# The first batch of a retention kernel: pairs of heads over 512 tokens in place of groups of four heads over 256

## The chip, the cores and the metric

The kernel runs on one core of one Trainium2 chip. Its time is the device time of one execution in microseconds (us). Before the change three runs gave a median of 301.55 us (301.51 to 302.88).

## The reference

A multi-head retention layer is followed by a feed-forward layer. There are 8 batches, 8 heads, 576 tokens and a head size of 64, all in float32.

```python
scores = q @ k.T / sqrt(64)                       # per batch and head, 576 x 576
gamma  = 1 - 2.0 ** (-5 - head)
ret    = scores * (gamma ** (i - j) if i >= j else 0)
attn   = ret @ v                                  # 576 x 64
x      = attn, heads side by side                 # 4608 x 512
h      = x @ w_in                                 # 4608 x 2048
g      = where(h > 0, h, exp(min(h, 0)) - 1)
out    = g @ w_out                                # 4608 x 512
```

Since the decay is a product of a factor of the query's position and one of the key's, q and k are scaled by those factors once. The sequence is then cut into chunks: inside a chunk the masked scores are multiplied with v, and what lies ahead of a chunk comes in through a state, the sum of (scaled k) x v over the earlier tokens, a 64 x 64 matrix for each head.

## The kernel before

All matmuls take bf16 and add up in float32. `w_in` and `w_out` are loaded once, with a cast to bf16 in the transfer, by eight transfers of 512 columns or rows each (`load_w_in`, `load_w_out`), which GpSimd (POOL) issues. All loads of q, k and v and all stores are issued by SyncE (SP).

An *item* is 256 tokens (`T` = 0 or 1) of four heads (`w` = 0 or 1) of one batch, so that a batch has four items for its first 512 tokens; the last 64 tokens of four batches at a time are handled as two tail items. In items 0 to 11 a partition holds two neighbouring tokens (512 B runs in memory); from item 12 on one token (256 B runs). An item goes through these steps, named as in the code:

- `ldq`, `ldk`, `ldv`: loads of 256 KB (`load_main`, L405).
- `cq`, `ck`: scaling with the decay factors in halves, one for each of the two tokens of a partition (`scaled`, L476), on DVE or POOL; `cv`: cast of v (`cast_v`, L511).
- `T`, `cp`: for the first items, four TensorE transposes for q and four for k (L524) and a copy from PSUM (`turn_pe`, L530).
- `sc`: scores in chunks of 64 partitions, as 64x64 tiles of the array (`do_scores`); `mask`: causal mask on DVE (L851).
- `st`: two state increments, one for each 64-partition chunk (`do_state`); `mid`, `end`: running sums of them on DVE or ACT (L748 to L757); `bm`, `be`: these sums laid out as block-diagonal bf16 matrices (L765, L779).
- `iv`: queries times states and masked scores times v, in one PSUM accumulation (`do_inter`, `do_values`); `xc`: two copies to the transposed activations `xt` (`put_x`, L907).

A *block* is what the feed-forward layer takes at once. The first three batches (`NARROW`) have two blocks of 256 tokens each, the others one of 512; the tails are one more. `ffn1` multiplies `xt` with `w_in` (a narrow operation does two columns of 128 with 256 tokens each, a wide one 128 columns with 512 tokens), then ACT takes the exponential (L1045), ACT or DVE the maximum with 0 (L1053, L1055), and DVE joins both to `g` (L1060). `ffn2` multiplies `g` with `w_out`; the result is copied and stored.

The order of all this is not written by hand. Each step is an `Op` with dependencies, a rank and an estimated cost on each engine that may run it, and `Plan.run` lays them out on the engines when the kernel is built; the instructions are then issued in that order, and every engine works through its own in order. Constants steer it: `FROM` holds the earliest times at which the eight weight transfers may be issued, `HOLD` makes the loads from item 4 on wait for a piece of the weights (a one-element memset on POOL, L414, which waits for the transfer and which the load waits for), `ON` fixes engines, `RANKS` shifts ranks. The first two blocks' `ffn1` are planned together, four operations of each to a piece of `w_in`. TensorE begins with ten matmuls of zeros (`emit_warm`), and where the plan has a gap before 50 us, the code that issues the instructions puts matmuls or transposes of zeros into it (L1219).

The decay factors come from positions (`pos_i`, iota on POOL), `expo` (DVE, L298) and three exponentials on ACT (`emit_factors`, L1148), ahead of the first item. The causal mask of the items is built on POOL (L317).

Of the kernel before, what the change touches and what calls it, by code (L numbers as in the profile page):

```python
# [36 lines left out]
class Plan:  # L37
# [30 lines left out]
    def run(self, began):  # L68
# [58 lines left out]
        while len(order) < len(self.ops) or any(wire.values()) or events:  # L127
# [53 lines left out]
            for e, h in heads.items():  # L181
                h[1] -= step * rate[e]
                if h[1] < 1e-6:
                    wire[e].pop(0)
                    lanes[e] -= 1
                    heapq.heappush(events, (now + LEAVE, next(count), h[2]))
# [7 lines left out]
ENTER, LEAVE = 1.25, 0.55  # L194


LEAD = 64
HOLD = {4: "wi0"}
RANKS = {}
TOGETHER = 1  # L200
# [7 lines left out]
FROM = (8.96, 10.28, 13.13, 15.23, 17.0, 17.0, 17.44, 17.82)  # L208
ON = {'mid1': 'DVE', 'be2': 'DVE', 'md_1_0': 'ACT', 'xc1_2': 'DVE', 'cv0': 'DVE', 'md_1_1': 'ACT', 'cq12': 'DVE'}
DIRECT = True  # L210
# [5 lines left out]
TWO = False  # L216
# [18 lines left out]
def kernel(  # L235
# [45 lines left out]
    for h in range(H):  # L281
        nc.vector.memset(lgt[:, h : h + 1], lg[h])
    pos_i = const.tile([P, NU], I32, name="pos_i")
    nc.gpsimd.iota(pos_i[:, :FT].rearrange("p (t e) -> p t e", e=2), pattern=[[2 * P, 2], [1, 2]], base=-MID,
                   channel_multiplier=2)
    nc.gpsimd.iota(pos_i[:ST, FT:], pattern=[[0, 1]], base=FT * P - MID, channel_multiplier=1)
    nc.gpsimd.iota(pos_i[ST:, FT:], pattern=[[0, 1]], base=MID - FT * P, channel_multiplier=-1)
    pos = const.tile([P, NU], FP32, name="pos")
    nc.vector.tensor_copy(pos, pos_i)
# [3 lines left out]
    nc.vector.memset(bk, 0.0)  # L293
    bt = const.tile([P, 1], FP32, name="bt")
    nc.vector.memset(bt[:ST], math.log(scale))
    nc.vector.memset(bt[ST:], 0.0)
    expo = const.tile([P, NU, H], FP32, name="expo")
    nc.vector.tensor_tensor(  # L298
        expo,
        pos.unsqueeze(2).to_broadcast([P, NU, H]),  # L300
        lgt.unsqueeze(1).to_broadcast([P, NU, H]),
        ALU.mult,
    )
# [8 lines left out]

    mask = const.tile([P, 2, 2, C], BF16, name="mask")
    nc.vector.memset(mask, 1.0)
    for c in range(2):
        m = mask[c * C : (c + 1) * C]
        nc.gpsimd.affine_select(out=m, in_=m, compare_op=ALU.is_ge, fill=0.0, base=0,  # L317
                                pattern=[[-1, 2], [1, 2], [2, C]], channel_multiplier=-2)
    mask_t = const.tile([P, ST], BF16, name="mask_t")
    nc.vector.memset(mask_t, 1.0)  # L320
# [3 lines left out]
    nc.vector.memset(diag[D:, 1:], 1.0)  # L324

# [20 lines left out]
    for b in ORDER:  # L346
        for r in range(FT if isinstance(b, int) else 1):
# [4 lines left out]
            else:  # L352
                it.b, it.T, it.w = b, r // 2, r % 2
                it.blk = 2 * b + it.T if b < NARROW else 2 * b
# [903 lines left out]
```

## Time and profile before

| | |
|---|---|
| median of three runs | 301.55 us |
| the profiled execution | 301.8 us, of which the span from its first to its last instruction 300.1 us |
| TensorE matmuls busy | 291.5 us (97%) |
| ScalarE (ACT) busy | 188.2 us (63%) |
| VectorE (DVE) busy | 172.3 us (57%) |
| GpSimd (POOL) busy | 164.4 us (55%) |
| HBM read and written | 36.70 MB, 9.44 MB |
| first `ffn1` matmul | at 19.06 us |
| first `ffn1` matmul of batch 1 | at 50.40 us |
| granted TensorE clock | 1.00 |

The profile is of one execution; all times in it count from its first instruction. In lists of instructions a line has start, length, engine, line of the kernel, operation, output and input names, shape and number; a bracket behind it names idle time of the engine just before and what ended it. PE is TensorE, DVE VectorE, ACT ScalarE, POOL GpSimd, SP SyncE; PEld is the loading of weights into the array, which overlaps with matmuls. A "q" behind an engine is its instruction queue. Lengths of matmuls in a row are modelled and reach a little past the start of the next ones, so that the start times are the better measure. In a table of windows the columns are the stretch, its length and busy time of PE, PEld, DVE, ACT and POOL, then TensorE clock, share of the DMA engines and GB/s.

### The profile page before, as it was taken

How to read it: one execution, taken by the hardware profiler on the slowest of the kernel's cores; microseconds unless marked ns; L12 is line 12 of the kernel's file. 1: busy time of each engine (PE TensorE's matmuls, PEld its weight loads, DVE VectorE, ACT ScalarE, POOL GpSimd, SP SyncE). 2: the span in 40 equal slices, each digit the busy share in tenths (PEclk: the TensorE clock that was granted, in tenths of full speed). 3: DMA queues.
4: the chain of work that ended last, by engine and by line, in shares of the span. 5: the costliest groups of instructions: out<-in, count | busy, mean ns of one | idle time of the engine just before them, and what ended most of it. 6: DMA issues, size and time to landing. Idle time of an engine off the chain costs nothing.

```text
span 300.1 us, 8496 instructions
## 1 busy us (share of the span) xinstructions
PE 291.5 (97%) x3367; PEld 169.5 (56%) x3402; DVE 172.3 (57%) x312; ACT 188.2 (63%) x365; POOL 164.4 (55%) x292
## 2 busy tenths in 40 slices
PE   8899999999999999999999999999999999999996
PEld 4678746768767764545544554554545444444444
DVE  4888934948865537696843675646442474334300
ACT  2439724838766656786776667676764686777611
POOL 5790389984988849598794888579330000000000
DMA  6999999999998998999999999976761101011132
GB/s 201 272 207 210 226 292 316 231 260 184 179 238 183 217 205 193 219 191 212 192 224 165 173 231 208 186 176 106 175 142 72 35 0 38 35 35 37 35 106 70
DMA packets 135607, 50.10 MB, mean 167 GB/s; under 512 B 108176, under 2 KB 131088, under 8 KB 135568
## 3 DMA queue, kind: packets, MB, share of 16 engines
q1 hardware_dynamic: 131344, 45.37, 71.0%
q0 software_dynamic: 4224, 4.19, 8.4%
q8 instruction: 26, 0.43, 0.6%
q14 instruction: 13, 0.11, 0.1%
HBM read 36.70 MB, written 9.44 MB: 154 GB/s over the span
## 4 chain that ended last, share of the span: by engine, by line
PE 92%; DMA 2%; SPq 2%; issue 1%; POOL 1%; DVE 0%; ACT 0%; ACTq 0%
PE f L269 89%; PE sc L269 3%; DMA rqk<-in_q_dram 2%; SPq L405 2%; POOL qkn L476 1%; PE f L524 1%; POOL w_in_sb L454 0%; DVE xt L907 0%; ACT ot L1094 0%; ACTq L1094 0%
## 5 line engine op out<-in xcount | busy, mean ns | idle before, releaser
L1060 DVE SCALAR_TENSOR_TENSOR g<-e,f 128x512 bf16<-128x512 f32 x144 | 96.3, 685 | 79.3 <-ACT f L1053 78.7
L269 PE MATMUL f<-w_out_sb,g 128*128 128x512 bf16 (+2 forms) x582 | 136.9, 367 | 2.7 <-issue 1.9
L269 PE MATMUL f<-xt,w_in_sb 128*128 128x256 bf16 (+1 forms) x759 | 138.8, 325 | 0.6 <-DVE xt L907 0.2
L1045 ACT ACTIVATE e<-f 128x512 f32<-128x512 f32 x144 | 85.4, 596 | 48.0 <-PE f L269 41.6
L269 PEld LDWEIGHTS <-w_in_sb 128*128 128x128 bf16 x768 | 74.1, 98 | 53.2 <-DVE xt L907 0.5
L269 PEld LDWEIGHTS <-g 128*128 128x128 bf16 x608 | 56.7, 98 | 58.3
L1053 ACT ACTIVATE f<-f 128x512 f32<-128x512 f32 x122 | 72.2, 593 | 0.0
L818 POOL TENSOR_TENSOR s_mid<-mid,diag 128x256 bf16<-128x256 f32 x60 | 35.6, 613 | 12.9 <-DVE mid L807 7.9
L1094 ACT COPY ot<-f 128x512 f32<-128x512 f32 (+2 forms) x38 | 21.4, 566 | 22.6 <-PE f L269 22.6
L476 POOL TENSOR_TENSOR qkn<-rqk,far_q 128x256 bf16<-128x256 f32 x40 | 23.8, 613 | 5.5 <-DMA rqk<-in_q_dram 5.4
L476 POOL TENSOR_TENSOR qkn<-rqk,far_k 128x256 bf16<-128x256 f32 x40 | 23.9, 613 | 0.4 <-DMA rqk<-in_k_dram 0.2
L511 POOL CAST vn<-rv 128x512 bf16<-128x512 f32 x28 | 17.0, 610 | 7.3 <-DMA rv<-in_v_dram 7.3
L476 POOL TENSOR_TENSOR qkn<-rqk,gq 128x256 bf16<-128x256 f32 x21 | 13.1, 635 | 12.1 <-DMA rqk<-in_q_dram 12.1
L907 ACT CAST xt<-f 128x256 bf16<-128x256 f32 x24 | 9.2, 425 | 14.1 <-PE f L269 14.1
L851 DVE TENSOR_TENSOR pt<-sc,mask 128x1024 bf16<-128x1024 f32 x12 | 14.6, 1219 | 4.3 <-PE sc L269 4.2
L845 DVE TENSOR_TENSOR pt<-sc,mask_t 128x1024 bf16<-128x1024 f32 (+1 forms) x12 | 12.5, 1042 | 5.7 <-PE sc L269 4.2
L1055 DVE TENSOR_SCALAR f<-f 128x512 f32<-128x512 f32 x22 | 15.2, 695 | 0.9 <-ACT e L1045 0.6
L579 POOL TENSOR_TENSOR qkt<-rqt,gq 128x256 bf16<-128x256 f32 x16 | 9.5, 613 | 10.6 <-DMA rqt<-in_k_dram 10.6
L883 ACT CAST xt<-f 128x512 bf16<-128x512 f32 x16 | 8.6, 589 | 10.2 <-PE f L269 9.5
L476 POOL TENSOR_TENSOR qkn<-rqk,gk 128x256 bf16<-128x256 f32 x22 | 13.3, 621 | 2.4 <-DMA rqk<-in_k_dram 2.4
L818 POOL TENSOR_TENSOR s_end<-end,diag 128x256 bf16<-128x256 f32 x20 | 12.3, 613 | 0.4 <-DVE end L807 0.3
L807 DVE TENSOR_TENSOR mid<-f,mid 128x256 f32<-128x256 f32 (+1 forms) x24 | 9.1, 380 | 2.5
(81 smaller groups left out, 170.7 us busy)
## 6 DMA issues: line engine op xcount, KB each, us to landing
out_dram<-ot SPq DMA_DIRECT2D x30, 256.0 KB, 3.0
rqk<-in_q_dram SPq DMA_DIRECT2D x40, 128.0 KB, 3.4
rqk<-in_k_dram SPq DMA_DIRECT2D x40, 128.0 KB, 3.3
rv<-in_v_dram SPq DMA_DIRECT2D x40, 128.0 KB, 3.1
rqk<-in_q_dram SPq DMA_DIRECT2D x12, 256.0 KB, 5.8
rqk<-in_k_dram SPq DMA_DIRECT2D x12, 256.0 KB, 5.4
rv<-in_v_dram SPq DMA_DIRECT2D x12, 256.0 KB, 6.9
w_in_sb<-in_moe_w_in_dram POOLq DMA_DIRECT2D x4, 512.0 KB, 8.8
```

The source lines that it names most:

```text
L269: pin(nc.tensor.matmul(*a, **kw))
L476: pin(alu[op.eng].tensor_tensor(tiles[key][:, i, e], tiles[raw][:, :, e], g, ALU.mult))
L511: pin(copy[op.eng](tiles["vn", n], tiles["rv", n]))
L579: pin(alu[op.eng].tensor_tensor(tiles["qkt", n, m, j][:, hs], tiles["rqt", n, m, j][:, hs], g[:, hs], ALU.mult))
L818: pin(alu[op.eng].tensor_tensor(tiles[out].rearrange("p h (j d) -> p h j d", j=2), tiles[key][:, i].unsqueeze(2).to_broadcast([P, 2, 2, D] ...
L845: pin(nc.vector.tensor_tensor(tiles[it.pt].rearrange("p i h n -> p (i h n)")[:, : 2 * w * C].rearrange("p (i x n) -> p i x n", i=2, n=C), ...
L851: pin(nc.vector.tensor_tensor(tiles["pt", n].rearrange("p i h n -> p (i h) n"), tiles[it.sc].rearrange("p i (h n) -> p (i h) n", h=2), mas ...
L1045: pin(nc.scalar.activation(tiles[ekey], tiles[hkey], AF.Exp))
L1053: pin(nc.scalar.activation(ph, ph, AF.Relu))
L1055: pin(nc.vector.tensor_scalar_max(ph, ph, 0.0))
L1060: pin(nc.vector.scalar_tensor_tensor(tiles[gkey], tiles[ekey], -1.0, tiles[hkey], ALU.add, ALU.min))
L1094: pin(copy[op.eng](tiles[okey][:, :cols], tiles[pkey][:, :cols]))
```

## The change

The first 512 tokens of batch 0 are cut in another way. Its four items are now the four pairs of heads, each over all 512 tokens, with four neighbouring tokens in a partition (1 KB runs). Everything that they do is new (`quad`):

- Scaling is still in halves, of two tokens to a partition each. The factors are those of `quad_pos` (four positions for a partition), computed ahead of the first item; those of the other batches, and their mask, are built by steps of their own (`near_i`, `near_x`, `near_f`, `mask_n`) that batch 1 waits for.
- A chunk is 32 partitions (128 tokens). Scores take 32 matmuls for 16, with 64 rows and 32 columns of the array each; the mask `quad_m` has four rows of 32 partitions.
- The states are summed over the chunks by TensorE: four running sums in one PSUM tile, over 32, 64, 96 and 128 partitions, in 40 matmuls for 16 (a part of 96 partitions is made of 64 and 32), with a drain of TensorE ahead of the last eight. One copy (`sm`) takes the four sums to bf16; `mid`, `end` and `bm` of these items are gone. `be`, on POOL, is now needed for the tail only.
- Values take 32 matmuls with 32 rows and 64 columns each; the three states of chunks 1 to 3 come in by six matmuls with 64 rows, half a head pair each; a drain stands ahead of the last 16.
- Two copies put an item into `xt`, for one pair of heads over 512 tokens.

Batch 0 is thus one block of 512 tokens: wide `ffn1`, four row groups in `ffn2` (two at a time, `OPEN`), and a store in which a row group has every fourth token. The loads come in the order of `SEQ`. The weights may be issued from other times (`FROM`; the first piece from 7.2 in place of 8.96), the loads of batch 1 wait for the first piece of `w_out` in place of `w_in` (`HOLD`), seven warm-up matmuls stand for ten, and the fillers are of 512 columns where a gap is long. `RANKS` and `ON` get many entries; the estimate of transfers gets a lag (`LAG`).

```diff
-HOLD = {4: "wi0"}
-RANKS = {}
-TOGETHER = 1
+HOLD = {4: 'wo0'}
+RANKS = {'ck04': 3, 'cp(5, 0)': -1, 'st4b1': -8, 'xc0_4': 0.5, 'iv4b0': 0.5, ...}
+OPEN = 2
...
+SEQ = 'q0 k0 q1 k1 v0 q2 k2 v1 q3 k3 v2 v3'
+WARM = 7
+WEIGHTS = "wi0 wi1 wi2 wi3 wo0 wo1 wo2 wo3"
...
-FROM = (8.96, 10.28, 13.13, 15.23, 17.0, 17.0, 17.44, 17.82)
-ON = {'mid1': 'DVE', 'be2': 'DVE', 'md_1_0': 'ACT', 'xc1_2': 'DVE', 'cv0': 'DVE', ...}
+FROM = (7.2, 7.9, 12.0, 16.3, 9.9, 12.3, 6.3, 18.0)
+ON = {'be3': 'ACT', 'cv2': 'ACT', 'cp(1, 0)': 'ACT', 'cp(2, 1)': 'ACT', 'cq12': 'DVE', ...}
...
+            if it.early:
+                def emit_quad(op, src=src, key=key):
+                    pin(nc.sync.dma_start(
+                        tiles[key].rearrange("p a b d -> p (a b d)").rearrange("p (h r) -> p h r", h=2),
+                        src[0, 2 * it.j : 2 * it.j + 2, : FT * P, :].rearrange("h (p e) d -> p h (e d)", e=4)))
...
+            if it.early:
+                es = slice(2 * e, 2 * e + 2)
+                pin(alu[op.eng].tensor_tensor(
+                    by_token(tiles[key][:, i])[:, es], by_head(tiles[raw])[:, :, es].rearrange("p h e d -> p e h d"),
+                    (quad_q, quad_k)[i][:, es, 2 * it.j : 2 * it.j + 2].unsqueeze(3).to_broadcast([P, 2, 2, D]), ALU.mult))
+                return
...
+    def quad(it):
...
+        def emit_sc(op):
+            tt = tiles["qkT", n]
+            for m in range(4):
+                for i in range(2):
+                    for cs in chunk:
+                        mm(tiles[sc_key][cs, i, m * P : (m + 1) * P].rearrange("p (e t) -> p e t", e=4),
+                           tt[half[i], 7 - m, cs], tt[half[i], 0:4, cs], start=True, stop=True)
...
+        def emit_st(op):
+            o, kn, vn = tiles[skey], by_token(tiles["qkn", n][:, 1]), by_head(tiles["vn", n])
+            for kind, lo, hi in ((0, 0, 1), (1, 0, 2), (2, 0, 2), (3, 0, 4), (2, 2, 3)):
+                rows = slice(lo * QC, hi * QC)
+                if lo:
+                    pin(nc.tensor.drain())
+                for e in range(4):
+                    for i in range(2):
+                        acc(skey, 0, i, o[half[i], kind * D : (kind + 1) * D], kn[rows, e, i], vn[rows, i, e])
...
+            def values(cs):
+                for m in range(4):
+                    for c in cs:
+                        for i in range(2):
+                            acc(xkeys[c % 2], 0, i, tiles[xkeys[c % 2]][half[i], c // 2 * P : (c // 2 + 1) * P],
+                                vn[chunk[c], i, 3 - m], pt[chunk[c], i, m * P : (m + 1) * P])
+
+            values((0, 1))
+            for c in (1, 2, 3):
+                for i in range(2):
+                    acc(xkeys[c % 2], 0, i, tiles[xkeys[c % 2]][half[i], c // 2 * P : (c // 2 + 1) * P].rearrange(
+                        "p (e t) -> p e t", e=4), sums[half[i], j, c - 1], tt[half[i], 0:4, chunk[c]])
+            pin(nc.tensor.drain())
+            values((2, 3))
...
+    def emit_near_f(op):
+        pin(nc.scalar.activation(gq[:, :FT], expo[:, :FT], AF.Exp, bias=bq))
+        pin(nc.scalar.activation(gk, expo[:, :FT], AF.Exp, bias=bk, scale=-1.0))
+        pin(nc.scalar.activation(gq[:, FT], expo[:, FT], AF.Exp, bias=bt))
...
     def emit_warm(op):
-        for _ in range(10):
+        for _ in range(WARM):
             mm(tiles["warm"], zero[:, :P], zero, start=True, stop=True)
...
+    pieces = WEIGHTS.split()
+    for n, (name, t) in enumerate(zip(pieces, FROM)):
+        named[name].at = t
+        if n:
+            named[name].turn.append(named[pieces[n - 1]])
```

More of the change, by code (lines that the diff above doesn't have):

```diff
@@ L215 @@
 AWAY = {}
-TWO = False
 LAST = (0, 256, 384, 512)
@@ L1124 @@
         far_ready[0].at = 22.0
-    for it in items:
+    for word in SEQ.split():
+        load_main(items[int(word[1])], word[0])
+    for it in items[FT:]:
         (load_tail if it.tail else load_main)(it)
```

235 lines of the change are left out of this document (152 added, 83 removed).

## The prediction

> **What bounds the kernel now.** I read the page first: busy shares, slices, chain.
>
> ```profile
> PE 291.5 (97%) x3367; PEld 169.5 (56%) x3402; DVE 172.3 (57%) x312; ACT 188.2 (63%) x365; POOL 164.4 (55%) x292
> ...
> PE 92%; DMA 2%; SPq 2%; issue 1%; POOL 1%; DVE 0%; ACT 0%; ACTq 0%
> ```
>
> TensorE is the bound. But its 97% contain matmuls of zeros that fill waits, so I listed its instructions in order of time up to 40 us.
>
> ```profile
> 1.26 4.28 PE L269 MATMUL f<-zero 128*128 128x512 bf16 x10 [1.26 <-DVE zero L274]
> ...
> 15.78 1.07 PE L1219 MATMUL f<-ident,zero 128*128 128x128 bf16 x16
> ...
> 19.06 1.05 PE L269 MATMUL f<-xt,w_in_sb 128*128 128x256 bf16 x8
> ...
> 20.61 1.38 PE L269 MATMUL f<-xt,w_in_sb 128*128 128x256 bf16 x11
> 22.19 10.33 PE L269 MATMUL f<-xt,w_in_sb 128*128 128x256 bf16 x93 [0.21 <-DVE xt L907]
> ```
>
> The reader is to see two regimes. Before 19 us TensorE works in bits between fillers (operand zero): the attention of the first four items. From 22.19 us it is dense: the chain from there to the end holds no wait longer than 0.2 us ahead of the last output copies. So time is saved or lost where the dense stretch begins, or where something tears a hole into it. In 22.19 to 34.33 us lie 109 narrow matmuls less one group of transposes (0.22): 0.109 each. The 19 run earlier are worth 2.1 us, so the first FFN1 stands as if it had begun at 22.19 - 2.1 = 20.1 us.
>
> What sets that start is in the chain in order of time:
>
> ```profile
> 7.04 7.02 DMA rqk<-in_q_dram
> 14.06 0.07 issue
> 14.13 0.85 POOL qkn L476
> 14.98 0.75 POOL w_in_sb L454
> 15.73 0.02 issue
> 15.76 1.22 POOL qkn L476 x2
> ```
>
> The last item's q lands at 14.06; its k is scaled from 15.76, behind an issue of weights on POOL; FFN1 follows. Landings (issue plus time to landing, asked for each load): k of item 0 4.5, q of item 1 7.2, q and k of item 2 9.95 and 10.86, q of item 3 14.06, v of item 3 15.97; first w_in piece 9.08 + 8.9 = 17.98. One 256 KB load takes 0.92 us up to 11 us, then 1.6 beside the weights. In the windows:
>
> ```profile
> 6.00:8.00 2.00, 1.99 (x58) 1.74 (x56) 1.44 (x4) 0.20 (x1) 0.65 (x3) 1.00 1.16 316
> ...
> 18.00:20.00 2.00, 2.00 (x47) 1.62 (x48) 1.87 (x5) 0.08 (x1) 1.98 (x4) 1.00 1.22 201
> ```
>
> The last columns are clock, DMA share and GB/s: the DMA engines are full in both, first with loads, then with weights.
>
> **The change, part by part.** The sum is made against the profiled execution, 301.8 us (span 300.1 and 1.7 around it), 0.25 above the median 301.55.
>
> *Loads.* Runs grow from 512 B to 1 KB, 256 packets for 512 in each load; k of item 3 is the tenth, ahead of the last two v. Price of a packet: 512 B, 0.92 us x 16 engines / 512 = 29 ns. A weights packet (2 KB read): a piece in about 2.45 us (0.524 MB at 214 GB/s), 528 packets: 74 ns. A line through both gives 44 ns for 1 KB, 0.70 us a load. Bounds: 0.92 (nothing gained) and 0.61 (the weights' rate). I take 0.70, since 512 and 2048 B enclose it. From 4.5 us for the second load, plus 0.9 that the third and fourth cost extra before (7.2 - 4.5 - 2 x 0.92), the ninth lands at 4.5 + 0.9 + 7 x 0.70 = 10.3. The first weights may now be issued from 7.2 instead of 8.96, so they are in the wire by then; with the ratio 1.6 / 0.92 the tenth takes 1.2: 11.5 us.
>
> *Chain behind it.* FFN1 is wide now: it needs all four items. Before, ck of item 3 started at 15.76 and its values at 19.94: 4.2 us. Only one half of k stays on POOL (0.61 less): 3.6. Ahead of it half a mask on DVE, 0.6. The scores become 32 matmuls for 16: between nothing (twice the tiles at once) and 0.35 (16 took 0.35, 17.97 to 18.32), I take 0.15. Values and states: 32 + 6 matmuls at 0.35/16 = 22 ns, 0.83, and a drain. Drains are in no row: at least nothing (they only add), at most the 0.17 by which four transposes, 0.39 us, outlast their spacing of 0.22; I take 0.17, so 1.0. Copy to xt 0.45 and hand-overs 0.15; work of item 2 in front 0.3. FFN1 starts at 11.5 + 0.6 + 3.6 + 0.15 + 1.0 + 0.6 + 0.3 = 17.8 us against 20.1: -2.3.
>
> *State sums on TensorE.* Sixteen state matmuls become 40 and one drain; at 16 ns (16 in 0.25 us, 17.24 to 17.49) 0.63 + 0.17 = 0.8 us an item. It lies under the DVE mask (1.22), on nobody's path unless TensorE is full. Removed on DVE and POOL: mid, end and their blocks, some 14 instructions of 0.3 to 0.6; they ran while item 3 waited for its load, so only the DVE queue ahead of mask 3 gains, which the 0.6 above assumes.
>
> *Wide first block.* 64 matmuls of 512 at 0.216 (eight in 1.73, 58.24 to 59.97) are 13.85 us, 128 narrow ones 14.0: -0.15. FFN2 is the same work, its output rows still 2 KB.
>
> *Warm-up, factors, masks.* Seven warm matmuls at 428 ns end near 4.3 us; with ten the slow spell lasted to 5.5, so a microsecond of small work runs at half speed, hidden behind the landings. The factors of the other batches and their mask, and all that scales batch 1 or the tails and so waits for them, move behind the start: POOL iotas and selects about 1.3 us (covered until batch 1 lands; POOL idles 8 us from 22), DVE 0.6, ACT 0.9. During FFN1 ACT has no cover, it is busy 4.00 of 4 us from 30 to 34; the six PSUM buffers are it. Bounds 0 and 0.9; I take 0.3, nearer nothing, since a lag there is only paid when FFN2 starts.
>
> *Order.* Ranks, engines and release times of batch 0 are set anew; this decides which wait ends last, within the 0.6 and 0.3 above (bounds 0 and a whole mask, 1.2, for each). DVE's list for batch 0 (twelve scales at 0.34 back to back, four masks at 1.14, five copies) is 10.4 us, and fits before 14.2.
>
> *Batch 1.* Its loads wait for the first w_out piece instead of w_in.
>
> ```profile
> 19.08 3.03 POOL L462 DMA_DIRECT2D w_out_sb<-in_moe_w_out_dram x4
> 22.07 0.15 POOL L414 MEMSET rqk<- 128x1 f32 x1
> ```
>
> That memset on POOL lets SP load; POOL's scales and all later loads on SP stand behind it. Before, the first w_out piece landed at 29.1, so loads may start about 6 us later, near 28. DMA is full then (share 1.2), so the order changes, not the total: items 4 and 5 before came by 41.9 (26.83 + 15.1), sharing with w_out; now two pieces and six loads are left near 29.7: 4.9 + 6 x 0.92 = 10.4, so 40. From v of item 5 to its FFN1 was 8.5 us (41.9 to 50.40): 48.5, needed at 17.8 + 27.7 + 4.1 of attention between (the transposes, scores, states and values of 32 to 50 us) = 49.6. Cost 0, cover 1 us.
>
> Sum: -2.3 - 0.15 + 0.3 = -2.15: 299.65 on the profiled execution, **299.4** on the median.
>
> **Rivals.**
>
> *No gain from longer runs.* At 0.92 the eighth load lands at 10.9 and two more at 1.6 at 14.1; FFN1 starts at 20.4: +0.3 - 0.15 + 0.3, so 302.0, no change. For it: the DMA engines were as full at 316 as at 201 GB/s, which is share, not packet cost; against: 29 and 74 ns for a four times longer packet. By the Trainium skill ("DMA: Bandwidth & Descriptors", Specifications) line rate needs only 512 B, so doubling the runs would win nothing and the time would be that of this rival; the packets' two prices here don't agree.
>
> *TensorE fills the opening.* An item needs 0.44 (transposes) + 0.5 + 0.8 + 1.0 = 2.75 us, four 11, in the 12.4 from 5.4 to 17.8. If scores and states take 22 ns a matmul it is 0.44 + 0.7 + 1.05 + 1.0 = 3.2 and TensorE is full; at 3.5, start 19.4 and 301.0: no change. From 4.0 us an item (start 21.4) it is slower, at 4.7 (0.44 and 110 matmuls at 36 ns, two drains) start 24.2 and 305.8. For it: each switch from 64x64 work back to the full array shows 0.16 us idle (61.21). Against: 16 matmuls of 64x64 run in 0.25 to 0.35 us, so tiles do overlap. The Trainium skill ("TensorEngine Tiling (Array Packing)", Key Properties) says that a change of tiling mode drains the array; that speaks against this change, which has several shapes in an item.
>
> *Batch 1 late: slower.* Past 1 us of delay each further one is a hole in the dense stretch; from w_out landing near 33 instead of 28 it decides (hole 4), at 35 the hole is 6 and the time 305.4. For it: the four w_out pieces took 10 to 17 us to land. Against: they shared with the loads that now wait.
>
> *More gain.* Loads at 0.61 and an idle DVE: start 16.4, 298.1.
>
> **How the numbers follow.** Under 0.5% (1.5 us) a measurement of this kernel can't be told from no change. Forecast (298.5 to 300.0) 0.47; more gain 0.11; no gain from runs 0.15; TensorE mildly full 0.10; badly full 0.08; batch 1 late 0.09. Faster 0.47 + 0.11 = 0.58, same 0.25, slower 0.17. The range 297.6 to 302.6 takes in start times from 16 to 21 and leaves out the two slow cases; the likeliest one's own is 298.5 to 300.0.
>
> **What would show it.** Landing of k of item 3 near 11.5, spacing of loads near 0.7; first FFN1 matmul on 512 columns near 17.8, none of width 256 before batch 1; states with their drain near 0.8 us. Wrong if loads keep 0.9, if TensorE shows no fillers between 8 and 16 us, or if it idles near 46 to 52 us, waiting for xt of batch 1.

## The result and the profile after

The changed kernel takes 316.88 us (median, 316.66 to 318.88); the kernel before ran at 301.53 us beside it. The ratio is 1.0515 (95% interval 1.0462 to 1.0568): 5% slower, where 299.4 us (297.6 to 302.6) was forecast. The profiled execution took 316.9 us with a span of 315.2, against 300.1 before, so 15.1 us have to be found.

Busy time of the engines and the chain by engine, from the page of the changed kernel:

```profile
PE 302.5 (96%) x3510; PEld 166.8 (53%) x3510; DVE 172.5 (55%) x303; ACT 192.8 (61%) x377; POOL 161.3 (51%) x295
...
PE 91%; DMA 4%; POOL 2%; issue 1%; DVE 1%; SPq 1%; ACT 0%; ACTq 0%
```

TensorE still seems to be busy all the time, but it gained 11 us of busy time though the feed-forward work is the same, and DMA and POOL have gained 2 and 1 points of the chain. Both halves of the loss show in TensorE's instructions in order of time (start, length, number, in brackets the wait ahead):

```profile
12.48 0.33 PE L275 MATMUL f<-pt,vn 32*64 32x128 bf16 x9
...
13.18 0.29 PE L275 MATMUL f<-pt,vn 32*64 32x128 bf16 x5
15.07 0.53 PE L275 MATMUL f<-pt,vn 32*64 32x128 bf16 x11 [1.61 <-issue]
...
18.81 1.79 PE L275 MATMUL f<-vn,qkn 32*64 32x64 bf16 x38
21.05 0.26 PE L275 MATMUL f<-vn,qkn 32*64 32x64 bf16 x2 [0.45 <-issue]
21.24 0.62 PE L275 MATMUL sc<-qkT 64*32 64x128 bf16 x32
...
27.34 4.95 PE L275 MATMUL f<-xt,w_in_sb 128*128 128x512 bf16 x13
...
72.08 0.48 PE L275 MATMUL sc<-qkT 64*64 64x128 bf16 x16 [2.92 <-DMA qkT<-qkn]
```

*Opening.* The first FFN1 matmul runs at 27.34 instead of the 20.1 that the first of before is worth: 7.2 us late. From about 9 us on TensorE has work almost without a break, and it is full of matmuls of 32 rows or columns: no filler stands between 10.5 and 26.3 us. Twice it stands still in the middle of a row of the same matmuls, for 1.61 and 0.45 us, with nothing in the profile that it waits for ("issue"). FFN1 then takes 15.8 us, where 64 matmuls at the full clock would take 13.85, and FFN2 starts at 43.14 instead of 34.33: 8.8 us of the 15.1.

*Second half.* Around 70 to 80 us the dense stretch has a hole, which it did not have before: waits of 2.92, 0.61 and 1.04 us, and a stretch at half clock behind them. That is most of the other 6.3 us.

Windows of the changed kernel, then of the kernel before (stretch, length, busy time of PE, PEld, DVE, ACT, POOL, then clock, DMA share, GB/s):

```profile
14.00:32.00 18.00, 16.00 (x297) 9.83 (x298) 5.11 (x8) 5.05 (x12) 4.63 (x8) 0.53 0.77 121
20.00:30.00 10.00, 9.16 (x176) 5.47 (x173) 1.65 (x2) 2.47 (x7) 4.63 (x8) 0.50 0.46 66
50.00:60.00 10.00, 10.00 (x182) 5.79 (x181) 6.06 (x11) 3.94 (x10) 5.79 (x11) 1.00 0.65 176
```

```profile
20.00:30.00 10.00, 9.79 (x104) 8.40 (x103) 8.38 (x17) 9.20 (x20) 2.22 (x4) 1.00 1.22 209
50.00:60.00 10.00, 9.95 (x79) 7.62 (x79) 6.99 (x12) 7.39 (x14) 10.00 (x19) 1.00 1.23 256
```

The clock is 0.53 of full speed on average from 14 to 32 us: the rest of the opening and the first 4 us of FFN1 run at half speed. And the DMA engines, which were full in both windows before (1.22 and 1.23), fall to 0.46 and 0.65. Summed up over windows of 10 us, 14.67 MB had moved by 60 us before the change and 11.91 MB after it. POOL's list shows the first of these two gaps:

```profile
13.43 0.41 POOL L1062 TENSOR_TENSOR blocks<-sums,diag 128x128 bf16<-128x128 bf16 x1
21.80 0.40 POOL L1062 TENSOR_TENSOR blocks<-sums,diag 128x128 bf16<-128x128 bf16 x1 [7.96 <-ACT sums L1057]
24.13 0.40 POOL L1062 TENSOR_TENSOR blocks<-sums,diag 128x128 bf16<-128x128 bf16 x1 [1.93 <-ACT sums L1057]
24.47 0.81 POOL L473 DMA_DIRECT2D w_in_sb<-in_moe_w_in_dram  x1
25.27 2.98 POOL L481 DMA_DIRECT2D w_out_sb<-in_moe_w_out_dram  x4
28.20 0.16 POOL L433 MEMSET rqk<- 128x1 f32 x1
```

The blocks `be` of items 2 and 3 (the last two `blocks` lines), which only the tail needs, stand on POOL ahead of the last piece of `w_in`, all of `w_out` and the memset that lets batch 1 load. They wait for sums that TensorE has not made. So the memset comes at 28.20, in place of 22.07.

### The profile page after: what moved, and what is told of

Its sections match the earlier page's. It is cut to its first block, busy times and chain, and to the rows that moved or that the text cites. A ratio compares the mean times of both kernels' runs of the same rounds, so it can differ in the third digit from the quotient of the medians.

```text
span 315.2 us, 8751 instructions
## 1 busy us (share of the span) xinstructions
PE 302.5 (96%) x3510; PEld 166.8 (53%) x3510; DVE 172.5 (55%) x303; ACT 192.8 (61%) x377; POOL 161.3 (51%) x295
## 4 chain that ended last, share of the span: by engine, by line
PE 91%; DMA 4%; POOL 2%; issue 1%; DVE 1%; SPq 1%; ACT 0%; ACTq 0%
PE f L275 87%; PE sc L275 3%; DMA qkT<-qkn 2%; POOL qkn L507 2%; DMA rqk<-in_q_dram 1%; PE f L555 1%; DVE qkn L503 0%; POOL vn L542 0%; SPq L424 0%; SPq L402 0%; DVE pos L1243 0%; ACT ot L1206 0%; DVE expo L1244 0%; SPq L594 0%; ACTq L1206 0%
## 5 line engine op out<-in xcount | busy, mean ns | idle before, releaser
L275 PE MATMUL f<-w_out_sb,g 128*128 128x512 bf16 (+2 forms) x608 | 142.6, 370 | 0.0
L275 PE MATMUL f<-xt,w_in_sb 128*128 128x512 bf16 (+1 forms) x704 | 140.7, 344 | 0.0
L275 PEld LDWEIGHTS <-w_in_sb 128*128 128x128 bf16 x704 | 68.7, 99 | 59.5 <-issue 2.5
L507 POOL TENSOR_TENSOR qkn<-rqk,gq 128x256 bf16<-128x256 f32 x14 | 8.6, 618 | 19.5 <-DMA rqk<-in_q_dram 19.5
L1165 DVE TENSOR_SCALAR f<-f 128x512 f32<-128x512 f32 x24 | 16.7, 695 | 1.8 <-ACT e L1155 1.6
L926 ACT CAST xt<-f 128x256 bf16<-128x256 f32 x20 | 7.4, 423 | 15.8 <-PE f L275 15.8
L869 DVE TENSOR_TENSOR pt<-sc,mask 128x1024 bf16<-128x1024 f32 x8 | 9.8, 1220 | 9.7 <-PE sc L275 9.7
L275 PE MATMUL f<-vn,qkn 64*64 64x64 bf16 (+2 forms) x608 | 14.2, 203 | 0.8 <-issue 0.4
L275 PE MATMUL f<-pt,vn 64*64 64x64 bf16 (+2 forms) x576 | 12.6, 223 | 2.0 <-issue 1.6
L275 PE MATMUL sc<-qkT 64*64 64x64 bf16 (+2 forms) x576 | 10.3, 216 | 4.0 <-DMA qkT<-qkn 4.0
```

The costliest lines, as they stand in the source:

```text
L275: pin(nc.tensor.matmul(*a, **kw))
L507: pin(alu[op.eng].tensor_tensor(tiles[key][:, i, e], tiles[raw][:, :, e], g, ALU.mult))
L869: pin(nc.vector.tensor_tensor(tiles["pt", n].rearrange("p i h n -> p (i h) n"), tiles[it.sc].rearrange("p i (h n) -> p (i h) n", h=2), mas ...
L1165: pin(nc.vector.tensor_scalar_max(ph, ph, 0.0))
```

## The experiments

Each ratio is to the kernel before on the same chip, with its 95% interval. "Changed" is the changed kernel. "Standstill" means here that TensorE waits for nothing that the profile shows; "the hole" is the group of waits near 70 to 80 us.

### Is it the standstill and the clock, or POOL's order?

The first theory: TensorE stands still, its clock halves, and the late sums hold POOL. Fillers ahead of the slow spots should keep the clock up; `be` behind the weights should free POOL; both together should do most.

```diff
+        for _ in range({'iv0': 8, 'st2': 7}.get(op.name, 0)):     # e1_fill, e3_both: 512 columns of zeros
+            mm(tiles[...], zero[:, :P], zero, start=True, stop=True)
...
+    for n in range(FT):                                           # e2_be_late, e3_both
+        named[f"be{n}"].turn.append(named["hold4"])
```

> Eight 512-column matmuls of zeros go ahead of the values of item 0 and seven ahead of the states of item 2, where TensorE stood still for 1.61 us (13.47) and 0.45 us (20.60) in the changed kernel. Theory A (the stalls are waits for the next block of TensorE's instructions, and it is the standstill at 13.5 us that lets the granted clock fall to 0.50 from 14.25 to 31.4): the idle time moves 16 instructions earlier in the stream and shrinks to 0.6 us or less, the clock stays at 1.00 through the opening, the first FFN1 matmul comes at 20 to 22 us instead of 27.3, and the FFN1 of the first block takes 14 us instead of 15.8. The hole near 70 us stays, since the weights and the loads of batch 1 still stand behind the blocks on POOL, but these come earlier by some 5 us with the states: 306 to 311 us. Rival B (the small tiles themselves don't count as work for the clock): the clock falls all the same by 18 us, FFN1 starts at 26 or later, 316 to 319 us. Rival C (the clock costs little, the late weights all): 315 to 317 us with the clock at 1.00.

> Only the order on POOL is changed: the four blocks of batch 0 (needed for the tail alone) go behind the issue of all weights and behind the memset that frees the loads of batch 1. Theory (the in-order wait of POOL for the states, 13.9 to 24.1 us, holds back the last w_in piece, w_out and batch 1, and makes the hole of 69 to 80 us): the last w_in piece is issued by 15 us, w_out by 18, the memset comes at 25 to 27 instead of 28.2, DMA no longer falls to nothing from 20 to 26 us; the hole near 70 shrinks by the 2 to 3 us by which the loads start earlier, with what it costs in clock: 311 to 314 us. The opening keeps its stall and its half clock, FFN1 starts at 27 as before. Rival (the hole comes from the order of batch 1's steps on POOL, not from the loads): hole as long as before, 316 to 317 us.

> Both edits. If the two causes are separate, their gains add: FFN1 starts at 20 to 22 us, the loads of batch 1 are issued at 25 to 27, no wait longer than 1.5 us between 46 and 90 us: 301 to 306 us. If they overlap (the blocks come earlier anyway once the clock holds), it is as the first of the two runs within 1.5 us.

Measured: e1_fill 318.34 us, 1.053 (1.042 to 1.065); e2_be_late 321.26 us, 1.063 (1.049 to 1.077); e3_both 321.99 us, 1.065 (1.047 to 1.084). All three missed: none gained anything over the changed kernel. In e1_fill the clock held from 15.5 to 25.7 us (window as above, then the middle of it):

```profile
14.00:32.00 18.00, 17.17 (x342) 9.67 (x343) 6.14 (x10) 6.13 (x15) 4.98 (x9) 0.86 0.80 125
15.50:25.50 10.00, 9.39 (x313) 6.13 (x312) 3.54 (x5) 2.92 (x8) 1.83 (x4) 1.00 0.59 99
```

but the fillers cost some 2.7 and 1.6 us of TensorE (the first group still ran at half clock), and FFN1 began at 26.91, 0.4 us earlier: what the clock gave, the fillers took. So TensorE is full there. At the full clock that run also gives the price of an item: transposes 0.46, scores 0.35, states 1.25, values with the states 1.13, together 3.2 us. In e2_be_late POOL was free (memset at 17.38, DMA share 1.2 from 14 to 42 us), yet FFN1 came later, at 31.86, with a new standstill:

```profile
22.59 0.26 PE L275 MATMUL f<-vn,qkn 32*64 32x64 bf16 x2 [0.45 <-issue]
28.95 0.31 PE L275 MATMUL f<-pt,vn 32*64 32x128 bf16 x1 [2.24 <-issue]
```

Part of that lateness is the clock, which was at a half from 7.4 us on here and not from 14.3. (x12_stores_late below has the opening of the changed kernel unaltered; in its profile the clock fell at 8.8 us and FFN1 came at 29.05.) But the new standstill is a clue: the changed kernel, whose DMA engines are nearly empty by then, has none there. Counting TensorE's matmuls from the start, the standstills come after 222 and 349 of them in the changed kernel, after 349 and 476 in e2_be_late, after 347 and 474 in e3_both: always 127 apart, whatever they compute. A matmul is two instructions here (a weight load and the multiplication), and two drains lie among the 127 from 222 to 349: 256 instructions.

### Fillers in the kernel before

If the clock falls when TensorE is not filled, the kernel before without its fillers should show it.

```diff
-            if gap > 0:
+            if False:
```

> The kernel before without the matmuls and transposes of zeros that fill the plan's gaps up to 50 us; nothing else is left out. If standing still is what lowers the clock (theory A), the granted clock falls to 0.50 between 8 and 16 us and stays there for some 10 us or more into FFN1; the half-speed opening and FFN1 cost 3 to 7 us: 304 to 309 us. If the small work of 64x64 tiles holds the clock by itself: clock 1.00, 301 to 302 us.

Measured: 303.84 us, 1.0058 (1.0021 to 1.0094). The clock was at 0.50 from about 9 to 22 us, as expected, but that cost some 1.5 us only, just less than the least expected: an opening that waits for loads can afford half a clock. That one full of matmuls cannot is the reading for the changed kernel; its price is estimated further down.

### Fewer state matmuls; other shapes; another engine for a block

```diff
-            for kind, lo, hi in ((0, 0, 1), (1, 0, 2), (2, 0, 2), (3, 0, 4), (2, 2, 3)):
+            for kind, lo, hi in ((0, 0, 1),):                     # x5_one_sum
...
-ON = {'be3': 'ACT',
+ON = {'be4': 'DVE', 'be3': 'ACT',                                  # x6_be4_dve, x7_merged
...
-                    for i in range(2):                             # x7_merged: 20 matmuls of 128 columns
-                        acc(skey, 0, i, o[half[i], kind * D : (kind + 1) * D], kn[rows, e, i], vn[rows, i, e])
+                    acc(skey, 0, 2, o[:, kind * P : (kind + 1) * P].rearrange("p (h d) -> p h d", h=2),
+                        kn[rows, e].rearrange("p h d -> p (h d)"), vn[rows, :, e])
```

x5 leaves out the running sums (the one state is copied into all four places), and so do x10, x14, x17 and x18 below: they show what these matmuls cost, not another way to get the result. In x7 two copies stand for the one that takes the sums to bf16.

> Leaves out the summing of states: only the state of the first 128 tokens is computed (8 matmuls an item for 40, no drain) and copied into all four sums. Theory A (TensorE, working through its instructions in order, is the bound of the changed opening: 3.2 us an item at full clock plus a standstill at every 128 matmuls): 128 matmuls fewer take away one block of instructions and 4 us at full clock, more where the clock is at half; the first FFN1 matmul comes at 20.5 to 23 us instead of 27.3, the hole near 70 stays: 309 to 313 us. Rival B (what the opening waits for are copies, masks and loads, TensorE only follows): FFN1 at 26 or later, 315 to 318 us.

> The block be of item 4 goes to DVE instead of POOL. Theory A (POOL, in order, waits 5 us, 49.2 to 54.2, for that item's end sum, with the scaling of items 6 to 8 behind it; that keeps load buffers, then SP, then the transpose of item 7 late): POOL works through from 46 us, the wait of 2.92 us at 72.08 and the two after it (0.61, 1.04) shrink to under 1.5 us in all, with the clock at 1.00: 311 to 314 us. Rival B (the transpose is late because the loads of batch 1 are issued 6 us later and queue in front of it on SP): the wait stays over 2 us, 316 to 318 us. The opening is as in the changed kernel.

> As the previous one, and the states of the two heads of a pair come from one matmul of 128 columns (20 matmuls an item for 40, of which only the two diagonal blocks are copied out, by two copies for one). Theory A (number of TensorE instructions counts in the opening): 80 matmuls fewer up to FFN1, but each takes 56 ns instead of 31, so the work in the states is the same 1.1 to 1.3 us an item; what is saved is the second standstill and some of the time at half clock: FFN1 at 25 to 27 us, 309 to 313 us. Rival B (time of the matmuls alone counts): FFN1 as before at 27 to 28, total as in the previous run within 1.5 us.

Measured: x5_one_sum 313.33 us, 1.0351 (1.0298 to 1.0403), FFN1 at 24.66 where 20.5 to 23 was expected, with a standstill of 1.57 after matmul 350; the direction is right, the size is not. x6_be4_dve 320.31 us, 1.058 (1.053 to 1.063): POOL's wait of 4.99 us for `be4` went, but POOL then stood 3.37 us ahead of the next such block, and TensorE waited 2.86 (at 68.62) and 4.60 us (at 83.55). x7_merged 322.05 us, 1.060 (1.052 to 1.068): half as many state matmuls and no standstill above 0.4 us, but FFN1 at 32.06. Its trace says why: the clock was at a half from 8.9 to 32.8 us, without any standstill ahead of it, and the 20 matmuls of an item took 2.7 us (21.97 to 24.69), where 1.1 to 1.3 had been expected and the 40 of the changed kernel took 1.25 at full clock. So fewer instructions are no gain where TensorE is full and each takes longer: in the opening of the changed kernel both count.

### Number of instructions, or time on TensorE?

The decisive pair is in the kernel before, where nothing else changes. In x8 each of the first four items gets 24 extra matmuls of 64x64 in unused columns; in x11 two of 512 columns, which take longer on the array (0.77 us for an item's row with them, 0.45 for that of x8).

```diff
+        if it.early:                                               # x8_before_more
+            for x in range(24):
+                hl, e, c, i = x // 8 % 2, x // 4 % 2, x // 2 % 2, x % 2
+                mm(tiles[views[c][0]][i * D : (i + 1) * D, 2 * P + hl * D : 2 * P + hl * D + D], kn[...], vn[...], ...)
...
+            for c in range(2):                                     # x11_before_long
+                mm(tiles[views[c][0]], kn[:, 1, 0, 0:2]..., vn[...], start=True, stop=True)
```

> The kernel before with 24 more state matmuls of 64x64 in each of its first four items (40 for 16, as many as the changed kernel has), written to unused columns: 96 matmuls, 192 TensorE instructions more. Theory A (instruction blocks of 128 matmuls cost a standstill where the work in them is small): a second standstill falls into the opening, FFN1 becomes dense 1 to 3 us later: 302.5 to 305 us. Rival B (the opening before has room for 1.5 us of small work): 301 to 302 us, the same.

> The control for the run with 24 more small matmuls: here the kernel before gets two more matmuls of 512 columns in each of its first four items, 0.43 us each pair, about the same TensorE time as 24 small ones (0.38 us), but 4 instructions for 48. Theory A (number of instructions): no second standstill in the opening, FFN1 dense at 20 to 20.8, 301.2 to 302.3 us. Rival B (TensorE time): the same loss as with the small ones, 303.5 to 305.5 us.

Measured: x8 305.43 us, 1.011 (1.005 to 1.017); x11 302.43 us, 1.004 (1.001 to 1.007). The intervals of the times overlap, so the traces have to decide. TensorE in x8:

```profile
13.41 0.22 PE L269 MATMUL f<-zero 128*128 128x128 bf16 x1 [0.61 <-issue]
...
16.95 0.38 PE L269 MATMUL f<-vn,qkn 64*64 64x64 bf16 x23
19.33 0.32 PE L269 MATMUL f<-vn,qkn 64*64 64x64 bf16 x17 [2.00 <-issue]
...
21.05 1.05 PE L269 MATMUL f<-xt,w_in_sb 128*128 128x256 bf16 x8
```

and the same stretch in x11:

```profile
17.15 0.84 PE L269 MATMUL f<-vn,qkn 128*128 128x512 bf16 x18
17.92 0.45 PE L269 MATMUL sc<-zero 128*128 128x128 bf16 x5
...
19.38 1.05 PE L269 MATMUL f<-xt,w_in_sb 128*128 128x256 bf16 x8
```

In x8 the 40 equal matmuls of an item are cut in two by 2.00 us, after the 351st matmul of the program, and an earlier standstill lies behind the 223rd: the same counts as in the changed kernel, in a kernel with other work. FFN1 is 2 us late, and 3 us are lost at the end. In x11 there is no standstill, and FFN1 starts at 19.38 (19.06 before). So these standstills come with the count, not with the time. TensorE's instructions come in blocks of 256, and one that is used up before the next is there makes it stand: between its two standstills x8 has 128 matmuls, 128 weight loads and no drain, 256 instructions as in the changed kernel. The transfers show it directly. In the trace of the kernel before the queue that carries instructions moves 0.43 MB in 26 transfers over the whole span, 16 KB each. In the changed kernel two of them end at 13.7 and 19.5 us, and the standstills end at 15.07 and 21.05; in x8 they end at 12.0 and 17.9, the standstills at 13.41 and 19.33. In each of the nine kernels that have such standstills, every one ends 1.3 to 1.6 us behind the end of a 16 KB transfer on that queue. Where two standstills follow each other, while loads and weights fill the DMA engines, the transfer of the second block begins 3.5 to 4.5 us after the block ahead of it was begun, and the block is usable after 5.9 to 6.9 (6.0 in the changed kernel, 5.9 in x8, 6.4 in e2_be_late, 6.9 in e3_both); when they are nearly empty (20 to 26 us in the changed kernel) the transfer began after 1.0 us, and the block needed at 476 was there in time. Dense feed-forward matmuls use a block in 14 us or more and never notice. The Trainium skill ("Runtime: NRT & Kernel Launch", Instruction fetch mechanics) has instructions come in blocks of 256 and calls the fetch mostly hidden: the count agrees with these runs, the hiding does not hold here.

The test in the other direction takes the changed kernel under that limit: four state matmuls an item and no fillers, some 335 matmuls up to FFN1 (some 314 before the change, some 500 in the changed kernel).

```diff
-            for kind, lo, hi in ((0, 0, 1), (1, 0, 2), (2, 0, 2), (3, 0, 4), (2, 2, 3)):
+            for kind, lo, hi in ((0, 0, 1),):
...
-                for e in range(4):
+                for e in range(2):
                     for i in range(2):
                         acc(skey, ...)
...
-            if gap > 0:
+            if False:
```

> Leaves out work: of the state sums only a part (4 matmuls an item for 40, as one state for all sums) and all fillers, so that TensorE has some 335 matmuls up to its first FFN1 instead of some 500. Theory A (a standstill at every 128th matmul, at 222 and 350, since the next 256 instructions come 6 us after the block before was begun while DMA is full): the one at 350 falls among FFN1's own long matmuls and is covered by them; no standstill marked issue over 0.4 us between matmul 222 and FFN1, FFN1 starts at 19.5 to 22.5 us; with the hole still there 308 to 312 us. Rival B (clock and waits for masks and copies set the start): FFN1 at 24 or later as with one sum.

Measured: 310.76 us, 1.0289 (1.0251 to 1.0328), as theory A has it. No standstill, FFN1 at 20.71 and FFN2 at 35.99 (34.33 before). The windows print a clock of 1.00 for this opening, but the profile has no clock for it ahead of 23.7 us, and the lengths speak against it (x10, then the same operations in e1_fill at full clock):

```profile
13.09 0.63 PE L275 MATMUL sc<-qkT 64*32 64x128 bf16 x32
13.65 0.64 PE L275 MATMUL f<-pt,vn 32*64 32x128 bf16 x16
```

```profile
17.13 0.42 PE L275 MATMUL sc<-qkT 64*32 64x128 bf16 x32
17.48 0.42 PE L275 MATMUL f<-pt,vn 32*64 32x128 bf16 x16
```

The 32 scores take 0.56 us up to the next row in x10 and 0.35 in e1_fill; in the changed kernel at half clock they take 0.55. So x10 went through its opening at half pace and was on time all the same: half a clock by itself does not make the opening late. Nor does x10 tell count from time. At half pace its 36 state matmuls less an item, 43 ns each (34 in 1.46 us in the changed kernel), are worth 6.2 us of TensorE, nearly all of the 6.6 by which FFN1 came earlier. For the count x8 against x11 and the transfers stand. Of the 15 us, 6 are gone with the opening's excess. The hole stayed (2.86, 0.99 and 1.03 us from 64.9 on), so it is not a result of the late opening alone.

### The hole

In the changed kernel the chain in order of time runs through the hole like this (start, length, what):

```profile
64.65 1.76 POOL qkn L507 x3
66.41 0.55 POOL vn L542
...
67.48 1.77 POOL qkn L507 x3
69.25 0.56 POOL vn L542
69.81 1.72 POOL qkn L507 x3
71.53 0.41 SPq L424
...
72.75 7.28 DMA qkT<-qkn
80.02 0.04 issue
80.07 0.42 PE sc L275 x16
```

POOL scales q and k and so frees buffers, SP issues the loads that waited for them, then a DMA transpose, and TensorE waits for the transposed item. Before, the first two transposes were issued at 52.23 and 56.31 and their scores ran at 60.29 and 63.90, 8.1 and 7.6 us later, without a wait; in the changed kernel these are 65.20 and 72.08, 72.75 and 80.07: 6.9 and 7.3 us later, with TensorE waiting at the end of both. Runs that take away one suspect each:

```diff
-PE_TURN = 7
+PE_TURN = 9                                                       # x9_pe_turn, from changed
...
+        if op.name.startswith("so_0_"):                            # x12_stores_late, from changed
+            op.turn.append(named["tr8"])
...
-HOLD = {4: 'wo0'}
+HOLD = {4: 'wi0'}                                                  # x13 from changed, x14 from x10
...
-HOLD = {4: "wi0"}
+HOLD = {4: "wo0"}                                                  # x16_before_hold_w_out, from before
...
+    for name, first in {'be4': 'ck16', 'bm5': 'ck16', 'be5': 'ck17'}.items():   # x17, from x10
+        named[name].turn.append(named[first])
...
-    "rqk": 7, "rv": 6, ...
+    "rqk": 9, "rv": 7, ...                                         # x18_more_buffers, from x10
```

> The changed kernel with items 7 and 8 of batch 1 and 2 transposed by TensorE and copied, as items 0 to 6 are, instead of by DMA. Theory A (the hole of 69 to 80 us is these two DMA transposes, issued late on SP and slow beside the loads: waits of 2.92 and 1.04 us and 1.8 us of half clock behind the first): no wait over 1 us between 60 and 80 us, 310 to 313 us. Rival B (what is late is POOL's scaling and the loads, the transposes only show it): a wait of 2 us or more stays there, for another tile, 315 to 318 us.

> The changed kernel with the four stores of block 0 put behind the transpose of item 8 on SP; nothing else. Theory A (loads and transposes stand behind stores that wait for FFN2 of block 0, so the DMA engines are only 0.6 busy from 52 to 64 us and the transpose of item 7 comes 3 us late): share over 0.8 from 50 to 62 us, wait at item 7 under 1 us, 311 to 314 us. Rival B (load buffers, freed by POOL, set the pace): share and wait as before, 316 to 318 us.

Measured: x9_pe_turn 320.06 us, 1.061 (1.057 to 1.065), and x12_stores_late 321.94 us, 1.065 (1.058 to 1.072). In both the wait moved to item 9: 6.83 us at 81.33 and 10.60 us at 86.11. (Some of what x12 lost lies in its opening, as said above.) Neither the transposes of items 7 and 8 by themselves nor block 0's stores are the cause.

> The changed kernel with the loads of batch 1 waiting for the first piece of w_in again, as before the change (one word in HOLD). The piece lands early, so what it changes is the order in which the work of batch 1 is written down: item 4's transposes, scores and states now stand around the start of FFN2 on TensorE, where they stood before the change, and no longer 28 FFN2 matmuls (6 us) behind it. Theory H (the second half of the loss comes from this order: item 4's states are late, its end block stands at the head of POOL's list and holds back the scaling of items 6 to 11, whose transposes are then late on SP): POOL waits less than 2 us for the end of item 4 (4.99 in the changed kernel), the waits of TensorE between 60 and 90 us for qkT fall from 2.9 and 1.0 to under 1 us together, 310 to 313 us with the opening as slow as it is. Theory I (the hole follows from the late opening or from the transfers, whatever the order): 316 to 318 us, waits of 3 us or more.

> The same one word in the kernel with 4 state matmuls an item and no fillers (its output is not the reference's: the running sums of batch 0 are left out), which had 310.8 us, 1.029 times the kernel before, with FFN1 at 20.71, FFN2 at 35.99 (before: 34.33) and a hole of 2.9 and 1.0 us from 64.9 on. Theory H: no wait above 1 us for qkT, POOL waits under 2 us for the end of item 4, 303 to 306 us (the 1.7 us by which FFN2 is late, and little else). Theory I: 309 to 311 us, the same hole.

> The changed kernel as it is, on the same chip as the two with the other order. Both theories: 315 to 319 us, FFN1 near 27.3, the hole of 2.9 and 1.0 us from 69 on.

> The kernel before with one part of the change alone: the loads of batch 1 wait for the first piece of w_out (HOLD), and the order of batch 1's work is planned by that. Nothing in the opening changes. Theory O (this order alone makes the hole): a wait of over 2 us for qkT between 55 and 85 us, 304 to 308 us. Theory D (what makes the hole is that transfers fall behind: the 16 DMA engines are full from 6 to 90 us in the kernel before, 14.7 MB moved by 60 us; a stop of POOL or of SP anywhere ahead costs the end of that stretch what it leaves empty): the time follows the megabytes moved by 60 us; the loads start at 22 us as before, so 14 MB or more and 301.5 to 304 us.

> The kernel with 4 state matmuls an item and no fillers (the running sums of batch 0 are left out, its output is not the reference's; 310.8 us, 13.5 MB moved by 60 us), with the end blocks of items 4 and 5 and the middle block of item 5 behind the scales of items 6 and 7 on POOL, so that POOL does not stand 3.6 us behind a block whose states are late. Theory D: POOL's idle time from 43 to 47 us goes, its buffers come free earlier, DMA share from 46 to 60 us rises from 0.7 to 0.9, the waits for qkT behind 60 us fall from 4 us to 2, 307 to 309 us. If the hole has nothing to do with POOL's stop: 310 to 312 us.

> The same kernel with two more buffers for raw q and k and one more for raw v (9 and 7 for 7 and 6), so that SP may load 0.75 MB further ahead while POOL stands. Theory D: 14 MB or more moved by 60 us, waits for qkT of 2 us or less, 306 to 309 us. If loads are not what is late: 310 to 312 us.

Measured: x15_changed_again 316.13 us, 1.049 (1.043 to 1.056), the same kernel on another chip. x13_hold_w_in 318.48 us, 1.058 (1.049 to 1.068), and x14_hold_under_block 313.99 us, 1.041 (1.037 to 1.044): x14 slower than x10 and x13 no faster than the changed kernel, though FFN1 of batch 1 started earlier (x13 at 56.90 us against 59.64 in x15, x14 at 51.75 against 53.78 in x10). The chain of x14:

```profile
57.19 5.27 DMA qkT<-qkn
62.46 0.04 issue
62.50 0.42 PE sc L275 x16
...
69.76 11.39 DMA qkT<-qkn
81.15 0.04 issue
81.20 0.64 PE sc L275 x16
```

What was won ahead of the hole was lost in it. Theory H (the order that comes from HOLD makes the hole) falls, and so does theory O, the same for the kernel before: x16 had 302.51 us, 1.000 (0.997 to 1.003), with 15.05 MB moved by 60 us, so the order that comes from HOLD costs nothing in the kernel before. x17 had 311.84 us, 1.032 (1.028 to 1.036), and x18 312.82 us, 1.035 (1.030 to 1.040). Both missed what theory D (late transfers make the hole) had expected, 307 to 309 and 306 to 309 us: POOL's stop did go in x17, but loads and scales then waited for each other in other places (DMA share 0.58 and 0.63 in 48 to 56 us), and the additional buffers of x18 brought one wait of 6.37 us in place of three.

What all these runs share is how much had been moved. By 60 us the kernel before and x16, both near 302 us, had moved 14.67 and 15.05 MB; x10, x14, x17 and x18, 311 to 314 us, had 13.27 to 13.56; the changed kernel, x9, x12 and x13, 316 to 322 us, had 11.91 to 12.42. Within the last group the order does not hold: x12 had moved the most and was the slowest. The others fit in: x8 had 14.02; e2_be_late, e3_both and x7, 321 to 322 us, had 11.24 to 11.65. The kernel before keeps its DMA engines full from 6 to 90 us, so it has nothing with which to make up a gap in the transfers. That the transfers set the pace behind 60 us fits all of this, but it is argued: a kernel that is late for any reason has also moved less. Which edit of the change makes the loads of batch 1 run behind in 40 to 60 us, when the opening is on time as in x10, stays open; a kernel without any DMA transposes in the stretch of the hole was not run.

## Why the prediction was wrong

**Loads: right.** The longer runs did what was forecast. From 8 to 12 us, when almost only loads were moved, 1390 packets took 16 engines at a share of 1.01 for 4 us: 47 ns each (44 forecast), 0.75 us a load (0.70). And item 3's k was scaled on POOL at 12.04 instead of 15.76. The rival *no gain from longer runs* fell, and with it the rule of the Trainium skill ("DMA: Bandwidth & Descriptors", Specifications) that 512 B already give line rate: here loads of 1 KB runs moved 341 GB/s in that stretch, and loads of 512 B runs 292 in the same stretch of the kernel before.

**State sums: the step that failed.** "It lies under the DVE mask (1.22), on nobody's path unless TensorE is full." TensorE was full. The 40 state matmuls and their drain took 1.25 us at full clock, 31 ns each, not 0.8; 16 ns had been taken from a row of 16 that overlapped well. With 3.2 us an item (2.75 forecast) alone the rival's own table gives a start near 18 us. What made it 27.34 is missing from the sum altogether. The number of TensorE instructions ahead of FFN1 went from some 628 to some 1000, and blocks of 256 came every 6 us (x8 against x11, and the transfers), which led to standstills of 2.1 us. And the clock was at a half from 14 to 31 us. What that cost can be estimated: from 15.07 to 26.31 us the changed kernel took 10.8 us besides its second standstill, and e1_fill took 7.1 us for the same instructions at full clock (16.9 to 25.55 without its fillers), so 3.7 us ahead of FFN1 and 2 us in it. These shares don't simply add up, since a faster TensorE reaches the end of a block sooner and waits longer there, and fillers that hold the clock up take the time they win (e1_fill). Why the clock fell stays open.

**The rival that came true, for another reason.** *TensorE fills the opening* had 0.18 in two parts, and from 4.7 us an item it asked for 305.8. From 5.4 to 27.34 us the opening took 5.5 us an item. Its mechanism, small tiles that don't overlap, was priced at up to 36 ns a matmul; measured at full clock were 31 for the states, 11 for the scores. The arrival of instructions wasn't among the rivals.

**Wide block: mis-sized by the clock.** The forecast 13.85 us for 64 matmuls became 15.8, as its first 4 us ran at half clock.

**Factors: right in kind.** They stepped in earlier than forecast, at 6.88 us ahead of item 1's k on DVE, 0.51 and 0.20 us on the chain, and no longer mattered.

**Batch 1: the second step that failed.** "Cost 0, cover 1 us." The loads did start near 28 (28.38), but behind POOL's blocks, not behind `w_out`, and the DMA engines stood nearly empty from 20 to 28 us, where "DMA is full then (share 1.2), so the order changes, not the total" had been assumed. FFN1 of batch 1 did not wait for its items, so the sign named for this case (idle near 46 to 52 us) did not come. The price came one step later, at the DMA transposes of items 7 and 8 (7 to 9 in other runs): about 6 us. The cover had been worked out for items 4 and 5 only. That the late loads are its cause is argued, as said above.

**Signs.** "No fillers between 8 and 16 us" was named as what would show the prediction wrong, and is what the trace shows, but for three short groups before 10.6 us.

## What to carry to other kernels

Cutting work into smaller tiles costs instructions, and on a stretch where the DMA engines are full TensorE here got 256 instructions (127 or 128 matmuls) in 6 to 7 us: count the matmuls of such a stretch, and not only their time. And check a clock that a table prints against the length of a known row of matmuls. Where the DMA engines are full for the whole first third, a part that is "moved behind the start" isn't free: price it by the bytes that are late, and follow it past the first items that have cover. Work for the end of the program (here `be`, which only the tail needs) does not belong on a queue ahead of issues that others wait for.

## What was not expected of the hardware

- TensorE stands still at fixed counts of instructions: after 222 or 223, 347 to 351 and 474 or 476 matmuls, in nine of the kernels, for 0.45 to 2.49 us, and goes on 1.3 to 1.6 us behind the end of a 16 KB transfer of instructions.
- The clock fell to a half 0.8 us into a standstill of 1.61 us in the changed kernel, in the kernel before without fillers from 8.5 to 22 us with waits of no more than 1.4 us, and in x7 from 8.9 us on with none above 1.14; yet x8 kept 1.00 through standstills of 0.61 and 2.00 us. Every stretch at half clock that begins and ends inside a profile lasts 3.41 us or a multiple of it, up to 27.3 us in e2_be_late. No single rule for when one begins comes out of these runs.
- A DMA transpose of one item took 4.5 to 5.1 us from issue to landing in the kernel before (50 to 80 us); those that TensorE waited for in the kernels that ran behind took 5.3 to 14.9 us (5.27 and 11.39 in x14, 14.92 in x12).
